# Where an expert's code converts the next expert's weights: six of eight pieces inside the arms of its branch, the third block's place, and two PSUM banks

## The chip, the core and the metric

One core of one Trainium2 chip runs the whole program. The metric is device microseconds of one execution. TensorE (PE) does matrix products into PSUM, VectorE (DVE) and ScalarE (ACT) read PSUM and convert, GpSimd (POOL) gathers and scatters rows by an index list, SyncE (SP) issues the loads of weights.

## What is computed

Chunked attention, a dense layer with `h * sigmoid(1.702 h)`, and a mixture of experts, on 1536 tokens of 512 features. Only the last part matters here:

```python
logits = x @ w_gate                      # 8 experts
expert_idx = np.argmax(logits, axis=1)
gate_w = probs[np.arange(N), expert_idx]
for i in range(N):                       # up to capacity = 384 tokens per expert
    disp[e, counts[e]] = x[i]
h = np.maximum(np.einsum('ecd,edf->ecf', disp, w1), 0.0)   # w1: 8 x 512 x 1024
y = np.einsum('ecf,efd->ecd', h, w2)                       # w2: 8 x 1024 x 512
out[i] = gate_w[i] * y[expert_idx[i], pos[i]]
```

How many tokens an expert has is known only while the program runs.

## The kernel before

**Experts and blocks.** The experts run one after the other, in the order `EORDER`; "expert 0" below is the first to run, "expert 7" the last. An expert's tokens stand in up to three blocks of 128 rows (0, 1 and the "third", number 2). Evaluated with the reference, the counts in running order are 224, 291, 128, 160, 256, 160, 189 and 128.

**Arms.** `others()` emits the code of experts 1 to 7. A branch on the count chooses the arm: *narrow* (`first_of_narrow`, 129 to 192 tokens: experts 3, 5, 6), *wide* (`wide_two`, 193 or more: experts 1 and 4), *lone* (`first_of_one`, up to 128: experts 2 and 7). The wide arm may run a third block (`third`), itself wide or small (up to 64 rows); of experts 1 to 7 only expert 1 has one, a small one with 35 rows. Expert 0 has code of its own (`after_first`). All engines take these branches; an arm's code that is not taken lies between the branch and its target. The arms stand in the order narrow, wide (with the third block's arms inside), lone, and the code that follows them is `next_trans` (PE transposes the next expert's two blocks, L879; ACT and DVE copy them to `xs`, L883 and L884), a second branch that sends block 1's output (`send_second`), `tail(0)` (PE's last 15 products of block 0) and `send(0)`.

**Weights.** A product in float32 is made of three passes over parts `hi` and `lo`, so each expert's w1 and w2, loaded as eight pieces of 512 KB (pieces 0 to 3 are w1, 4 to 7 are w2) into eight buffers `raw`, has to be converted: ACT writes `hi` (L311), DVE writes `lo = raw - hi` (L316) and so frees the buffer, and SP then starts the load of the same piece of the expert after next (L257). While expert e runs, the pieces of e+1 are converted. Six slots `w` hold converted weights, two pieces each: four slots belong to the running expert, so pieces 0 to 3 fit at once, and pieces 4 to 7 only after `w1_done()` has given back the running expert's two w1 slots.

**Where pieces are converted before.** Three of them (`KEEPS[0]`) inside each arm: in the narrow and wide arms behind feature chunks 1, 3 and 5 (`PUMPS`) of the eight chunks of layer 1, in the lone arm through `pump(0..3)`. The other five stand in `steps(1)`, behind `next_trans()` and ahead of the branch with `send_second`.

**Order.** `turned()` and `in_order()` fix the order on PE, ACT and DVE inside one stretch of code, `as_written()` that of the experts' outermost level. Code in one arm that stands in no such stretch, or in two different ones, is free for the scheduler to interleave. Each engine runs its own list in order; layer 1's results pass through four PSUM tiles of kind `h`.

**Narrow arm.** Per chunk: PE makes one PSUM tile (8 products, L1149 and L1151), ACT copies its low half (L1156), DVE adds (L1157), ACT and DVE make `hT` (L1137, L1138), POOL copies block 1's part to `hp` (L1140). Then come 9 products of block 0 (`head`, L1037) and 16 of block 1 that read `hp` (`small2`, L972).

Of the kernel before, what the change touches and what calls it, by code (L numbers as in the profile page):

```python
# [21 lines left out]
P = 128  # L22
# [10 lines left out]
FROM = 150  # L33
EV1 = 2
PUMPS = (1, 3, 5)
RAWS = 4
RT = (4, 7)
LOADS = 1000
# [1 line left out]
EARLY = 12  # L40
KEEP = 4
KEEPS = (3, 8, 8)
HEAD2 = 3
HALF = P // 2
PUMPS1 = (0, 1, 1, 0)
# [46 lines left out]
def kernel(  # L92
# [34 lines left out]
    F2 = F // P  # L127
# [721 lines left out]
    def expert_parts(e, ep, tp, cnt):  # L849
# [79 lines left out]
            flat = t.rearrange("p z c n -> p (z c n)")  # L929
            return flat[:, :flat.shape[1] // 2].rearrange("p (c z n) -> p c z n", z=2, n=HALF)  # L930

        def small_h(b):

            x = narrow(xs_of(b)[0])
            h = narrow(hT_of(b))
            with in_order():
                ps = psum("h", "pst")
                for c in range(KC):
                    nc.tensor.transpose(ps[:, c * HALF:(c + 1) * HALF], xr[b][:HALF, c * P:(c + 1) * P], ident[:HALF, :HALF])
                pv = ps[:, :KC * HALF].rearrange("p (c n) -> p c n", n=HALF)  # L940
                nc.scalar.activation(out=x[:, :, 0], in_=pv, func=AF.Copy)
                nc.vector.tensor_tensor(out=x[:, :, 1], in0=pv, in1=x[:, :, 0].bitcast(F32), op=ALU.subtract)
                hs = []
                for j in range(2):
                    w_tile(("w1", e, j), 0)
                    w = w_tile(("w1", e, j), 1)
                    ps = psum("h", "psh")
                    for wz in range(2):
                        for c in range(KC):
                            nc.tensor.matmul(ps, lhsT=x[:, c].rearrange("p z n -> p (z n)"), rhs=w[:, wz, c, :],  # L950
                                             start=(wz, c) == (0, 0), stop=(wz, c) == (1, KC - 1))
                    hs.append(ep.tile([P, 512], F32, tag="hs", name="hs", bufs=2))
                    nc.scalar.activation(out=hs[j], in_=ps, func=AF.Copy)
                for j in range(2):
                    ps = psum("h", "psu")
                    for c in range(KC):
                        nc.tensor.matmul(ps[:, c * HALF:(c + 1) * HALF], lhsT=hs[j][:, c * P:(c + 1) * P], rhs=pair,
                                         start=True, stop=True)
                    hi, lo = (h[:, 4 * j:4 * j + 4, z] for z in range(2))
                    pv = ps[:, :KC * HALF].rearrange("p (c n) -> p c n", n=HALF)  # L960
                    nc.scalar.activation(out=hi, in_=pv, func=AF.Relu)
                    nc.vector.scalar_tensor_tensor(out=lo, in0=pv, scalar=0.0, in1=hi.bitcast(F32),
                                                   op0=ALU.max, op1=ALU.subtract)
# [62 lines left out]
        def y_of(b):  # L1026
            if b not in ys:
                ys[b] = psum(("y", "yl", "h")[b], "psy")
            return ys[b]
# [49 lines left out]

        begun = []  # L1080

        def begin():

            then = w_apart(e, KEEPS[0])
            if then is not None:
                begun.append(then)

        def end():

            if begun:  # L1090
                begun.pop(0)()

        def head(b):

            layer2_part(b, y_of(b), range(HEAD2))

# [4 lines left out]
        def first_of_one():  # L1101

            def pump(i):
                if i < 2:
                    begin()
                if i > 1:
                    end()

            with in_order():
                turn = block_h(0, pump)  # L1110
                begin()
                layer2_part(0, y_of(0), range(HEAD2 - 1))
                turn()
                end()
                layer2_part(0, y_of(0), range(HEAD2 - 1, HEAD2))

        def first_of_two():

            with turned():
                for fc in range(F2):  # L1120
                    layer1(fc)
                    end()
                    if fc in PUMPS:
                        begin()
                head(0)
                layer2_part(1, y_of(1), range(F2))

        def first_of_narrow():

# [12 lines left out]
            with turned():  # L1142
                for fc in range(F2):
# [14 lines left out]
                    if fc > 0:  # L1158
                        scale(fc - 1)
                    end()  # L1160
                    if fc in PUMPS:
                        begin()
                scale(F2 - 1)
                head(0)
                small2(1)

# [11 lines left out]
        def w1_done():  # L1178
            for j in range(F // 512):
                w_free(("w1", e, j))  # L1180

        def third_first(b, is_wide):

            if is_wide:
                trans(b, "h")
                block_h(b)()
            else:
                small_h(b)

        def third_second(b, is_wide):  # L1190

            gate(b)
            if is_wide:
                layer2_part(b, y_of(b), range(F2))
                send(b)
            else:
                small2(b)
                send_small(b)

        def third(b):  # L1200

            def go(is_wide):
                third_first(b, is_wide)
                ys.pop(b, None)
                third_second(b, is_wide)

            with tc.If(cnt[ex] > b * P):
                both(cnt[ex] > b * P + HALF, lambda: go(True), lambda: go(False))

        def wide_two():  # L1210

            first_of_two()
            third(2)

        def send_second(wide):

# [5 lines left out]
        def after_first():  # L1222

            y_of(0)
            with tc.If(cnt[E] < P) as some:
                load(0)
                trans(0)
                gate(0)
                block(0)
            with some.Else():  # L1230
                skip(0)
            gate(1)
            for b in range(2, NCB):
                load(b)
            first_of(1)
            assert NCB == 3
            y_of(1)
            hT_of(2)
            xs_of(2)
            third(2)  # L1240
            w1_done()
            layer2_part(1, y_of(1), range(F2))
            steps(1)
            send(1)

        def others():

            assert NCB == 3
            for b in range(2):
                y_of(b)  # L1250
                gate(b)
            for b in range(2, NCB):
                load(b)
                hT_of(b)
                xs_of(b)
            both(cnt[ex] > P, lambda: both(cnt[ex] < P + HALF + 1, first_of_narrow, wide_two), first_of_one)
            w1_done()
            next_trans()
            steps(1)
            with tc.If(cnt[ex] > P):  # L1260
                both(cnt[ex] > P + HALF, lambda: send_second(True), lambda: send_second(False))
            tail(0)
            send(0)

# [196 lines left out]
    with ExitStack() as st:  # L1461
# [4 lines left out]
        ps3 = st.enter_context(tc.tile_pool(name="ps_y", bufs=1, space=PSUM))  # L1466
        ps_pools["y"] = (ps3, "y", [P, 512])
        ps_pools["yl"] = (ps3, "yl", [P, 512])
        for kind in ("y", "yl"):
            psum(kind, "first")  # L1470
        ps2 = st.enter_context(tc.tile_pool(name="ps_h2", bufs=4, space=PSUM))
        ps_pools["t"] = (pst, "t", [P, 512])
# [104 lines left out]
```

## Time and profile before

| | us |
|---|---|
| median of 3 runs | 536.1 (534.67 to 537.48) |
| the profiled execution | 535.17 |
| its span, first to last instruction | 533.4 |
| PE busy in the span | 503.1 (94%) |
| DVE, ACT, POOL busy | 315.4, 277.3, 124.9 |
| stretch of experts 1 to 7 in the span | 365.5 to the end |

A wait in the profile is idle time of an engine and the event that ended it. "issue" means that the engine waited for nothing that the profile shows. [...]

### The profile page before, as it was taken

How to read it: one execution, taken by the hardware profiler on the slowest of the kernel's cores; microseconds unless marked ns; L12 is line 12 of the kernel's file. 1: busy time of each engine (PE TensorE's matmuls, PEld its weight loads, DVE VectorE, ACT ScalarE, POOL GpSimd, SP SyncE). 2: the span in 40 equal slices, each digit the busy share in tenths (PEclk: the TensorE clock that was granted, in tenths of full speed). 3: DMA queues.
4: the chain of work that ended last, by engine and by line, in shares of the span. 5: the costliest groups of instructions: out<-in, count | busy, mean ns of one | idle time of the engine just before them, and what ended most of it. 6: DMA issues, size and time to landing. Idle time of an engine off the chain costs nothing. (4 is left out here: it accounts for less than half of the span.)

```text
span 533.4 us, 10652 instructions
## 1 busy us (share of the span) xinstructions
PE 503.1 (94%) x4085; PEld 432.2 (81%) x4085; DVE 315.4 (59%) x637; ACT 277.3 (52%) x577; POOL 124.9 (23%) x131
## 2 busy tenths in 40 slices
PE   8799999999999999999999999999999979978885
PEld 3589789888998899989988888779887858867763
DVE  3999884588893282322256445538338848475761
ACT  2698886856652352222255334448328745465551
POOL 3245442332410031000000000153012822241402
PEclk9899999999999999999999999999999999999899
DMA  8788655041440004000059301499618958484401
GB/s 317 280 306 293 217 179 180 1 158 58 174 147 20 0 2 159 0 1 1 15 164 292 112 37 40 134 324 340 211 28 278 374 173 276 162 282 144 154 26 49
DMA packets 39155, 81.43 MB, mean 153 GB/s; under 512 B 3945, under 2 KB 10089, under 8 KB 39082
## 3 DMA queue, kind: packets, MB, share of 16 engines
q1 hardware_dynamic: 36010, 70.66, 38.9%
q0 software_dynamic: 3072, 9.80, 5.4%
q8 instruction: 45, 0.74, 0.6%
q14 instruction: 28, 0.23, 0.1%
HBM read 70.96 MB, written 9.75 MB: 151 GB/s over the span
## 5 line engine op out<-in xcount | busy, mean ns | idle before, releaser
L580 PEld LDWEIGHTS psh<-xT,w 128*128 128x128 f32 x1152 | 147.0, 188 | 8.2 <-ACT g L599 0.6
L623 PE MATMUL acc<-w,g 128*128 128x512 f32 x576 | 153.0, 400 | 0.0
L580 PE MATMUL psh<-xT,w 128*128 128x256 f32 x1152 | 151.7, 280 | 0.1
L623 PEld LDWEIGHTS acc<-w,g 128*128 128x128 f32 x576 | 100.6, 188 | 19.5 <-issue 2.1
L595 ACT ACTIVATE sg<-psh 128x256 f32<-128x256 f32 x96 | 36.7, 383 | 126.9 <-PE psh L580 126.4
L603 DVE TENSOR_TENSOR g<-sg,g 128x256 fp32r<-128x256 f32 x78 | 38.1, 490 | 80.3 <-ACT g L599 77.6
L316 DVE TENSOR_TENSOR w<-raw,w 128x1024 fp32r<-128x1024 f32 x64 | 75.8, 1222 | 5.8 <-ACT hs L1001 3.3
L311 ACT ACTIVATE w<-raw 128x1024 fp32r<-128x1024 f32 x64 | 64.5, 1055 | 0.1
L1037 PE MATMUL psy<-w,hT 128*128 128x512 f32 x240 | 59.7, 398 | 0.3
L1037 PEld LDWEIGHTS psy<-w,hT 128*128 128x128 f32 x240 | 43.9, 188 | 10.5 <-issue 0.9
L634 DVE SCALAR_TENSOR_TENSOR x<-acc,x 128x512 f32<-128x512 f32 x36 | 24.1, 685 | 20.8 <-PE acc L623 20.8
L599 ACT ACTIVATE g<-psh 128x256 fp32r<-128x256 f32 x96 | 36.2, 379 | 0.0
L1149 PE MATMUL psh<-xs,w 128*128 128x384 f32 x96 | 30.3, 354 | 3.9 <-DVE low L1157 3.9
L860 POOL DMA_INDIRECT xr<-rows,taker x23 | 28.6, 1245 | 12.6 <-issue 6.1
L758 POOL DMA_INDIRECT y<-rows,taker x1 | 1.2, 1219 | 123.8 <-DVE cnt_i L765 123.8
L884 DVE TENSOR_TENSOR xs<-pst,xs 128x512 fp32r<-128x512 f32 x14 | 9.0, 685 | 34.6 <-ACT xs L883 34.6
L883 ACT ACTIVATE xs<-pst 128x512 fp32r<-128x512 f32 x14 | 7.6, 596 | 38.8 <-PE pst L879 38.8
L1151 PE MATMUL psh<-xs,w 128*128 128x256 f32 x96 | 27.8, 289 | 0.0
L316 POOL TENSOR_TENSOR w<-w,w 128x512 fp32r<-128x512 f32 x12 | 16.6, 1387 | 44.0 <-ACT w L311 44.0
L1043 POOL DMA_INDIRECT out_dram<-y,taker x10 | 14.2, 1422 | 52.7 <-ACT y L1042 22.9
L281 ACT ACTIVATE w<-raw 128x512 f32<-128x512 f32 x32 | 21.3, 675 | 9.7 <-DMA raw<-in_w_out_dram 7.5
L306 POOL TENSOR_TENSOR w<-w,rest 128x512 int32<-128x512 int32 x13 | 17.4, 1338 | 36.3 <-DVE w L292 30.1
(163 smaller groups left out, 695.2 us busy)
## 6 DMA issues: line engine op xcount, KB each, us to landing
raw<-in_w_dram SPq DMA_DIRECT2D x64, 512.0 KB, 6.8
raw<-in_w_out_dram SPq DMA_DIRECT2D x16, 512.0 KB, 4.7
raw<-in_w_in_dram SPq DMA_DIRECT2D x16, 512.0 KB, 4.6
vt<-in_v_dram SPq DMA_DIRECT2D x12, 512.0 KB, 5.9
kt<-in_k_dram SPq DMA_DIRECT2D x12, 368.0 KB, 7.2
qt<-in_q_dram SPq DMA_DIRECT2D x12, 256.0 KB
out_dram<-blank SPq DMA_DIRECT2D x12, 256.0 KB, 2.7
rows<-x SPq DMA_DIRECT2D x5, 520.0 KB, 4.7
```

What stands on the lines that cost most here:

```text
L311: nc.scalar.activation(out=w_dst(self.name, self.i, 0), in_=w, func=AF.Copy)
L316: eng.tensor_tensor(out=lo, in0=w, in1=hi.bitcast(F32), op=ALU.subtract)
L580: nc.tensor.matmul(ps, lhsT=w[:, wz, c, i * P:(i + 1) * P], rhs=xT[tb][:, xz, c, :], start=n == 0, stop=n == 3 * KC - 1)
L595: nc.scalar.activation(out=sg_t[u], in_=h_t[u], func=AF.Silu, scale=1.702)
L599: g_last[:1] = [nc.scalar.activation(out=g[:, 0], in_=h_t.pop(u), func=AF.Silu, scale=1.702).ins]
L603: lo = eng.tensor_tensor(out=g[:, 1], in0=sg_t.pop(u), in1=g[:, 0].bitcast(F32), op=ALU.subtract)
L623: nc.tensor.matmul(acc_t[tb][s], lhsT=g[:, gz, s * P:(s + 1) * P], rhs=w[:, wz, wi, :], start=i == 0 and n == 0, stop=u == last_of(k, tb) ...
L634: nc.vector.scalar_tensor_tensor(out=dst, in0=acc_t[tb][s], scalar=1 / 1.702, in1=dst, op0=ALU.mult, op1=ALU.add)
L860: return nc.gpsimd.indirect_dma_start(out=t, out_offset=None, in_=rows[:, :], in_offset=bass.IndirectOffsetOnAxis(ap=taker[:, b, ex:ex + 1 ...
L1037: nc.tensor.matmul(ps, lhsT=h[:, hz, fc, o:o + P], rhs=w[:, wz, fc % 4, :], start=fc == 0 and n == 0, stop=fc == F2 - 1 and n == 2)
L1149: nc.tensor.matmul(ps[:, :2 * n].rearrange("p (z n) -> p z n", z=2), lhsT=w[:, 0, c, f0:f0 + P], rhs=t[:, :, c, :n], start=c == 0, stop=False)
L1151: nc.tensor.matmul(ps[:, :2 * P], lhsT=w[:, 1, c, f0:f0 + P], rhs=t[:, 0, c, :], start=False, stop=c == KC - 1)
```

## The change

- `PUMPS_N`: in the narrow arm only chunks 3 and 5 start a piece; behind the last chunk `w1_done()` and `more(IN_TWO)` convert pieces 2 to 5, ahead of `head(0)` in the text. Six pieces stand in that arm.
- The wide arm keeps its three pieces in layer 1 and has `more(IN_TWO)` at its end, pieces 3 to 5, in the same `turned()` as the last 15 products of block 1.
- The lone arm has four pieces (`IN_ONE`); two more stand in the new Else of the branch around `send_second`, which a lone expert takes.
- `steps(1)` (now two pieces) moves behind that branch.
- `third` gets an Else: the first 9 products of block 1 (`between`) run in whichever of its three arms is taken; in the wide and small ones behind the block's transposes.
- The PSUM banks of `y` and `yl` are swapped, by the order in which they are first taken.

```diff
+PUMPS_N = (3, 5)
+IN_TWO = 6
+IN_ONE = 4
...
-        def small_h(b):
+        def small_h(b, between):
...
                 nc.vector.tensor_tensor(out=x[:, :, 1], in0=pv, in1=x[:, :, 0].bitcast(F32), op=ALU.subtract)
+                between()
...
-        def begin():
-            then = w_apart(e, KEEPS[0])
+        def begin(keep=IN_TWO):
+            then = w_apart(e, keep)
             if then is not None:
                 begun.append(then)
+            return then
...
+        def more(keep):
+            while begin(keep):
+                if len(begun) > 1:
+                    end()
+            while begun:
+                end()
...
         def first_of_one():
             def pump(i):
-                if i < 2:
-                    begin()
-                if i > 1:
+                if i in (1, 2, 3):
                     end()
+                if i in (0, 1, 2):
+                    begin(IN_ONE)
             with in_order():
                 turn = block_h(0, pump)
-                begin()
+                begin(IN_ONE)
...
                 layer2_part(0, y_of(0), range(HEAD2 - 1, HEAD2))
+            w1_done()
...
                     if fc in PUMPS:
                         begin()
+                end()
                 head(0)
-                layer2_part(1, y_of(1), range(F2))
...
-                    if fc in PUMPS:
+                    if fc in PUMPS_N:
                         begin()
                 scale(F2 - 1)
+                w1_done()
+                more(IN_TWO)
                 head(0)
                 small2(1)
...
+        def third(b, between):
             def go(is_wide):
+                if is_wide:
+                    trans(b, "h")
+                    between()
+                    block_h(b)()
+                    gate(b)
+                    layer2_part(b, y_of(b), range(F2))
+                    send(b)
+                else:
+                    small_h(b, between)
+                    gate(b)
+                    small2(b)
+                    send_small(b)
+                ys.pop(b)
-            with tc.If(cnt[ex] > b * P):
-                both(cnt[ex] > b * P + HALF, lambda: go(True), lambda: go(False))
+            both(cnt[ex] > b * P, lambda: both(cnt[ex] > b * P + HALF, lambda: go(True), lambda: go(False)), between)
         def wide_two():
             first_of_two()
-            third(2)
+            third(2, lambda: layer2_part(1, y_of(1), range(HEAD2)))
+            w1_done()
+            with turned():
+                more(IN_TWO)
+                layer2_part(1, y_of(1), range(HEAD2, F2))
...
-            third(2)
+            third(2, lambda: layer2_part(1, y_of(1), range(HEAD2)))
             w1_done()
-            layer2_part(1, y_of(1), range(F2))
+            layer2_part(1, y_of(1), range(HEAD2, F2))
...
-            both(cnt[ex] > P, lambda: both(cnt[ex] < P + HALF + 1, first_of_narrow, wide_two), first_of_one)
-            w1_done()
+            before = w_state()
+            with tc.If(cnt[ex] > P) as some:
+                both(cnt[ex] < P + HALF + 1, first_of_narrow, wide_two)
+            two = w_state()
+            w_back(before)
+            with some.Else():
+                first_of_one()
+            one = w_state()
             next_trans()
-            steps(1)
-            with tc.If(cnt[ex] > P):
-                both(cnt[ex] > P + HALF, lambda: send_second(True), lambda: send_second(False))
+            w_back(two)
+            with tc.If(cnt[ex] > P) as some:
+                both(cnt[ex] > P + HALF, lambda: send_second(True), lambda: send_second(False))
+            two = w_state()
+            w_back(one)
+            with some.Else():
+                more(IN_TWO)
+            assert w_state() == two
+            steps(1)
             tail(0)
             send(0)
...
-        for kind in ("y", "yl"):
+        for kind in ("yl", "y"):
             psum(kind, "first")
```

What this does to the engines' lists is shown at three places.

**DVE, from the copies of `next_trans` on, expert 3.** `xs` are the next expert's transposed rows, `w` with `raw` is a piece's `lo`, `y` the output of block 1 of a narrow expert. Before:

```order
L884 TENSOR_TENSOR xs_6198<-pst_6758,xs_6198 128x4x128
L884 TENSOR_TENSOR xs_6198<-pst_6765,xs_6198 128x4x128
L316 TENSOR_TENSOR w5_4521<-raw1_3_3365,w5_4521 128x1024
L316 TENSOR_TENSOR w3_97<-raw2_0_4525,w3_97 128x1024
L316 TENSOR_TENSOR w3_97<-raw2_1_4526,w3_97 128x1024
L316 TENSOR_TENSOR w2_96<-raw2_2_4527,w2_96 128x1024
L316 TENSOR_TENSOR w2_96<-raw2_3_4528,w2_96 128x1024
L1260 COMPARE_AND_BRANCH
L1170 COMPARE_AND_BRANCH
L1170 UNCONDITIONAL_BRANCH
L978 TENSOR_SCALAR y_6794<-psy_6208,gt_6212 64x512
L979 SCALAR_TENSOR_TENSOR y_6794<-psy_6208,gt_6212,y_6794 64x512
```

After, from the second copy on:

```order
L887 TENSOR_TENSOR xs_6288<-pst_6894,xs_6288 128x4x128
L1277 COMPARE_AND_BRANCH
L1186 COMPARE_AND_BRANCH
L1186 UNCONDITIONAL_BRANCH
L982 TENSOR_SCALAR y_6908<-psy_6298,gt_6302 64x512
L983 SCALAR_TENSOR_TENSOR y_6908<-psy_6298,gt_6302,y_6908 64x512
L1186 UNCONDITIONAL_BRANCH
L319 TENSOR_TENSOR w3_97<-raw2_0_4525,w3_97 128x1024
L319 TENSOR_TENSOR w3_97<-raw2_1_4526,w3_97 128x1024
L1277 UNCONDITIONAL_BRANCH
L319 TENSOR_TENSOR w2_96<-raw2_2_4527,w2_96 128x1024
L319 TENSOR_TENSOR w2_96<-raw2_3_4528,w2_96 128x1024
```

Five pieces stood between the copies and the output `y`; now `y` follows the copies, a lone expert's two pieces stand in the other arm, and two pieces follow the branch.

**ACT, the beginning of the wide arm, expert 3's code (each expert has the same).** `w` with `raw1_3` is `hi` of piece 3, `raw1_0` and `raw1_1` those of pieces 0 and 1. Before:

```order
L1170 UNCONDITIONAL_BRANCH
L915 ACTIVATE hT_6199<-psh_6373 128x256
L915 ACTIVATE hT_6199<-psh_6388 128x256
L311 ACTIVATE w0_94<-raw1_0_3362 128x1024
L915 ACTIVATE hT_6199<-psh_6404 128x256
L915 ACTIVATE hT_6199<-psh_6421 128x256
L311 ACTIVATE w0_94<-raw1_1_3363 128x1024
```

After:

```order
L1186 UNCONDITIONAL_BRANCH
L314 ACTIVATE w5_4521<-raw1_3_3365 128x1024
L918 ACTIVATE hT_6289<-psh_6472 128x256
L918 ACTIVATE hT_6289<-psh_6487 128x256
L314 ACTIVATE w0_94<-raw1_0_3362 128x1024
L918 ACTIVATE hT_6289<-psh_6503 128x256
L918 ACTIVATE hT_6289<-psh_6520 128x256
```

Piece 3, in the text at the arm's end, has moved to the arm's first place, on ACT and likewise on DVE and in SP's list of loads. Pieces 4 and 5, which need the slots of `w1_done()`, stand behind the third block.

**PE, the small arm of the third block, expert 1.** `pst` are the transposes, `psy_4966` is block 1's output, `psh` layer 1 of the third block. Before:

```order
L1170 UNCONDITIONAL_BRANCH
L939 MATMUL pst_5364<-ident_64,xr_4955 128x64 x4
L950 MATMUL psh_5371<-w0_94,xs_4960 128x512 x8
L950 MATMUL psh_5382<-w5_4521,xs_4960 128x512 x8
L957 MATMUL psu_5393<-pair_88,hs_5380 128x64 x4
```

After:

```order
L1186 UNCONDITIONAL_BRANCH
L942 MATMUL pst_5376<-ident_64,xr_4973 128x64 x4
L1041 MATMUL psy_4966<-w3_97,hT_4957 128x512 x9
L954 MATMUL psh_5392<-w0_94,xs_4978 128x512 x8
L954 MATMUL psh_5403<-w5_4521,xs_4978 128x512 x8
L961 MATMUL psu_5414<-pair_88,hs_5401 128x64 x4
```

Nine products of block 1 now stand between the transposes and the layer 1 that waits for their copies.

## Rows read from the trace of the kernel before

**Rows 1.** Page: span, then two groups of section 5 (busy us, mean ns).

```profile
span 533.4 us, 10652 instructions
...
L316 DVE TENSOR_TENSOR w<-raw,w 128x1024 fp32r<-128x1024 f32 x64 | 75.8, 1222 | 5.8 <-ACT hs L1001 3.3
L311 ACT ACTIVATE w<-raw 128x1024 fp32r<-128x1024 f32 x64 | 64.5, 1055 | 0.1
```

**Rows 2.** Stretches of experts 1 to 6: length, busy by engine, PEclk, DMA share, GB/s.

```profile
365.50:400.10 34.60, 33.67 (x206) 29.48 (x205) 15.99 (x29) 13.91 (x29) 5.18 (x5) 1.00 0.50 169
400.10:413.98 13.88, 13.10 (x65) 10.52 (x64) 11.91 (x17) 12.34 (x21) 4.20 (x3) 1.00 0.89 280
413.98:438.75 24.77, 20.22 (x114) 17.71 (x112) 16.66 (x31) 14.34 (x32) 13.73 (x15) 1.00 0.78 283
438.75:463.82 25.07, 23.99 (x153) 21.27 (x152) 15.23 (x25) 12.36 (x24) 5.91 (x5) 1.00 0.65 215
463.82:489.35 25.53, 20.42 (x113) 17.62 (x112) 15.83 (x31) 14.62 (x33) 7.18 (x12) 1.00 0.65 207
489.35:514.62 25.27, 21.70 (x113) 19.01 (x112) 17.72 (x33) 14.65 (x33) 7.34 (x11) 0.93 0.38 131
```

**Rows 3.** Waits of PE, 340 to 533: total us, times, longest.

```profile
PE pst L879 <- issue: 7.3, 3, 3.6
PE psh L1149 <- DVE low L1157: 3.9, 3, 1.8
PE psy L972 <- POOL hp L1140: 1.8, 1, 1.8
PE psh L912 <- DVE hT L916: 0.9, 1, 0.9
PE psh L950 <- DVE xs L942: 0.9, 1, 0.9
PE psy L1049 <- ACT y L839: 0.8, 1, 0.8
PE psu L1006 <- ACT hs L1001: 0.8, 1, 0.8
```

**Rows 4.** Timeline of DVE, beginning of expert 3: start, us, instruction.

```profile
412.71 5.76 DVE L316 TENSOR_TENSOR w<-raw,w 128x1024 fp32r<-128x1024 f32 x5
...
419.32 0.62 DVE L1157 TENSOR_TENSOR low<-psh,low 128x192 f32<-128x192 f32 x2
```

**Rows 5.** Timeline, end of expert 3's arm: idle before in brackets.

```profile
429.19 0.29 POOL L1140 CAST hp<-hT 128x128 fp32r<-128x128 f32 x1 [0.27 <-DVE hT L1138]
...
434.28 1.06 PE L879 MATMUL pst<-ident,xr 128*128 128x128 f32 x8 [3.58 <-issue]
```

**Rows 6.** DMA queues within 430.5 to 434.5: packets, MB, share.

```profile
q8 instruction: 1, 0.02, 1.8%
```

**Rows 7.** Timeline of POOL, expert 4's sends and expert 5's copies.

```profile
466.78 2.05 POOL L1043 DMA_INDIRECT out_dram<-y,taker  x1 [9.82 <-ACT y L1042]
475.94 1.00 POOL L1043 DMA_INDIRECT out_dram<-y,taker  x1 [7.11 <-ACT hT L1137]
...
478.39 1.95 POOL L1140 CAST hp<-hT 128x128 fp32r<-128x128 f32 x8
```

**Rows 8.** Timeline of PE: expert 4's third-block branch; end of expert 5's arm.

```profile
451.39 1.33 PE L1037 MATMUL psy<-w,hT 128*128 128x512 f32 x5
452.87 6.77 PE L1037 MATMUL psy<-w,hT 128*128 128x512 f32 x28
...
484.94 1.07 PE L879 MATMUL pst<-ident,xr 128*128 128x128 f32 x8 [2.20 <-issue]
```

**Rows 9.** Timeline of PE, layer 1 of expert 1.

```profile
365.49 11.61 PE L912 MATMUL psh<-xs,w 128*128 128x256 f32 x96
```

**Rows 10.** Load issues of SP, 363.1 to 364.3.

```profile
L257 SPq DMA_DIRECT2D raw<-in_w_dram x1: 368/368/368, 364.1 to 364.1; - x1
```

**Rows 11.** DMA queues, 346.5 (first of these loads) to 369.0: packets, MB, share.

```profile
q1 hardware_dynamic: 2431, 4.70, 61.7%
```

More of the change, by code (lines that the diff above doesn't have):

```diff
@@ L1180, in w1_done @@
                 w_free(("w1", e, j))
[L1182 to L1200, printed above, removed]
-            def go(is_wide):
-                third_first(b, is_wide)
-                ys.pop(b, None)
-                third_second(b, is_wide)
-            with tc.If(cnt[ex] > b * P):
-                both(cnt[ex] > b * P + HALF, lambda: go(True), lambda: go(False))
+        def third(b, between):
+            def go(is_wide):
+                if is_wide:
[12 more added lines that the diff above has]
+            both(cnt[ex] > b * P, lambda: both(cnt[ex] > b * P + HALF, lambda: go(True), lambda: go(False)), between)
         def wide_two():
             first_of_two()
-            third(2)
+            third(2, lambda: layer2_part(1, y_of(1), range(HEAD2)))
[3 more added lines that the diff above has]
+                layer2_part(1, y_of(1), range(HEAD2, F2))
         def send_second(wide):
```

## The prediction

> **What bounds the kernel now.** I read the page first: a span of 533.4 us [rows 1], with PE busy for 94% of it by the table above. So only time in which PE idles can go, and the change touches experts 0 to 7 alone. The stretches by expert [rows 2] show where PE idles: subtracting its busy time from the length gives 0.9 us in expert 1, 1.1 in expert 4, 0.8 in expert 2, but 4.6, 5.1 and 3.6 in experts 3, 5 and 6, the three with a narrow arm; in expert 6 the granted clock is 0.93 besides. PE's waits [rows 3] give the causes, 16.4 us in all:
>
> - 3.9 us in three waits for DVE's first sums, at the start of experts 3, 5 and 6, the longest 1.8 (expert 6). DVE works through five pieces (5.76 us, so 1.15 each) before it reaches the first L1157 [rows 4], while PE fills the four PSUM tiles and stops. Expert 4 loses 0.9 in the same way (L916), expert 2 loses 0.8 because `hs` on ACT comes late behind five pieces of its own.
> - 1.8 us for POOL's `hp` in expert 5. Expert 4's second output is issued at 466.78 [rows 7], since ACT made its `y` only behind five pieces; the next send follows at 475.94, and the copies that PE wants start at 478.39.
> - 7.3 us "issue" at L879, the transposes behind the narrow arms: 3.58 [rows 5], 2.20 [rows 8], so some 1.5 in expert 6. Within expert 3's gap one 16 KB packet of queue q8, kind "instruction", moves [rows 6] (0.02 MB in the row). The branch out of a narrow arm jumps over the wide and the lone arm: by the listing 274 products of two instructions each, 548. I take the gap for the fetch of code. It begins when PE's sequencer has got past its last wait, POOL's last `hp`: that ends at 429.48 [rows 5] and 480.34 [rows 7], and PE resumes 4.80 and 4.60 us later, at 434.28 and 484.94. Of these PE still covers some with queued products.
> - 0.9 us for the third block's `xs` in expert 1, and 0.8 us in expert 0 for `y` of the block before (L1049), which lies in the bank that its dummy product writes.
>
> **The change part by part.** No product is added or taken away; pieces stay 64. So the sum consists of waits.
>
> *Fewer pieces at an expert's start.* Behind a narrow or wide arm DVE has two pieces instead of five between the copies and the next layer 1: 3 x 1.15 = 3.5 us earlier, more than any of the waits that it ends. Expert 4 gains 0.9, expert 5 1.1, expert 6 1.8. In a wide arm piece 3 comes in front, which leaves a net two pieces less (2.3), still enough for expert 4's 0.9. Behind a lone arm (expert 3) four pieces instead of five remain, 1.15 us against a wait of 0.97 (3.9 - 1.8 - 1.1): I take 0.7, between 0 and 1.0. Expert 2 gains its 0.8: ACT has two pieces (2 x 1.06 [rows 1]) where it had five. Its fourth piece in the arm stands between `turn(0)` and the second `hs`, where PE has six products to cover it.
>
> [...]
>
> *The send in front of the pieces.* `y` of block 1 no longer waits for five pieces, so expert 4's send is issued some 5 us earlier (5 x 1.06), and its successor, the gather and the copies with it. Expert 5 gains its 1.8 whole.
>
> *The narrow arm's end.* One piece less inside the loop and fewer ahead of it let DVE's last `hT`, and so the last `hp`, follow PE's last product of layer 1 more closely. In expert 3 PE ended its arm at 434.28 - 3.58 = 430.70, 1.2 us behind the last `hp`. Two pieces less on DVE are 2.3 us, PE itself comes 0.7 to 1.0 earlier, so the fetch begins some 1.5 us earlier in relation to PE's work: 1.6 gained of 3.58, bounds 0 and 2.2. The same for experts 5 (0.8 of 2.20) and 6 (0.6 of 1.5). The four pieces behind the loop take DVE 4.6 us and ACT 4.2, beside the 25 products of `head` and `small2` (5.8 us at 0.24 each) and the gap that remains: they end about when the transposes do. I cost them at nothing. If the cover is gone (the gap vanishes), the copies of `xs` start up to 1 us late, and `tail(0)`, 15 products or 3.6 us, still lies between them and layer 1.
>
> *The loads.* A piece converted earlier starts its load earlier. Between 400 and 414 DMA is 0.89 busy [rows 2], before that 0.50; so the shift goes into idle time. An expert wants 8 x 0.52 = 4.2 MB, 15 us at 280 GB/s [rows 2], and the six experts there last 24.9 us on average. The one place where this fails is piece 3 in front of expert 1's wide arm. Its buffer's load is issued at 364.1 [rows 10] as the ninth since 346.5; nine pieces are 4.72 MB, and q1 has moved 4.70 MB by 369.0 [rows 11]. With a little for the landing, ACT can convert it at 370.2, and everything on ACT's list waits, the first `hT` too. ACT ends at 371.3, DVE at 372.5, DVE's first `hT` at 372.9. PE has four PSUM tiles at 11.61 / 8 = 1.45 us [rows 9] and stops at 365.49 + 5.80 = 371.3. So **a new wait of 1.6 us**, bounds 0 (had the load been quicker) and 4. In expert 4 that load is some 5 us old by then, and nothing waits.
>
> *Third block.* In expert 1 nine products (2.2 us) now cover the 0.9 us: gained whole.
>
> *Banks.* Expert 0's 0.8 us may go, but expert 1's new wait is set by a transfer in a busy queue and takes back whatever is gained ahead of it. I count 0.
>
> *Lone entry.* The code of a lone arm is fetched under `tail(0)`; with more transfers beside it I take 0.4 as lost, bounds 0 and 0.8.
>
> [...] The branch past the third block (experts 0 and 4) now jumps over 122 products, 244 instructions, where it jumped over 208; 208 cost 452.87 - 452.72 = 0.15 us [rows 8]. [...]
>
> **The sum.** Expert 1: -1.6 + 0.9 = -0.7. Expert 2: +0.8. Expert 3: 0.7 + 1.6 = 2.3. Expert 4: 0.9. Expert 5: 1.1 + 1.8 + 0.8 = 3.7. Expert 6: 1.8 + 1.7 + 0.6 = 4.1. Lone entries: -0.4. Together 10.7 us gained. The profiled execution took 535.17 us, 1.8 more than its span, and would come to 524.5; the median of the three runs is 0.9 above it, so I forecast 536.1 - 10.7 = 525.4 us.
>
> **The rivals.**
>
> - *The waits move to the narrow arm's end.* The four pieces there issue four loads just when code is fetched, and hold ACT and DVE when the transposes come. Then the 7.3 us of "issue" stay (3.0 less gained), and so does the lower clock (1.7): 536.1 - 6.0 = 530.1. For it: expert 3's fetch, beside busy DMA, took 4.8 us. Against it: expert 5's took 4.6 with DMA less busy, so traffic matters little, and DVE's list gets shorter ahead of the last `hT`.
> - *Slower: the longer jump past the third block is out of reach.* Its place is the branch in experts 0 and 4. There PE has at most a few products queued, so each would cost a whole fetch, 4.7 us, and a stall of that size could bring the lower clock with it, 1.7 as in expert 6: 2 x 6.4 = 12.8, 536.1 - 10.7 + 12.8 = 538.2. It decides if the code that PE holds ahead ends between 208 and 244 instructions. For it: somewhere between 208 and 548 the reach ends. Against it: 244 is near the lower end. [...]
> - *It does not do what it says:* the sums at an expert's start wait for something else than the pieces (the second branch's join, say), the starts keep the 4.5 counted above (0.7, 0.9, 1.1, 1.8) and the clock its 1.7, while expert 1's loss remains: 536.1 - 10.7 + 6.2 = 531.6. DVE is busy until just before [rows 4], so I give it little.
> - *Expert 1's new wait brings the lower clock:* 1.7 more, 527.1; within the range.
>
> **How the numbers follow.** The forecast has 0.65 (the lower clock in expert 1 among it), the first rival 0.18, the slower one 0.07, the last but one 0.07; 0.03 for what I do not see. The range reaches down to 521.5 (expert 1 does not wait: 1.6; the gaps shrink by 1.5 to 2 us more, as their bounds allow) and up to 531.5, the first rival with 1.4 for a longer wait in expert 1 or at a lone entry. Half a per cent is 2.7 us, about what a measurement of this kernel can tell from no change. Faster by more than that (below 533.4) 0.86, within it 0.07, slower 0.07.
>
> **What would show it right or wrong.** In the waits of PE after: no L1149 or L916 counterpart at the starts of experts 4, 5, 6, at most 0.4 in expert 3; no `hp` wait; none for `hs` in expert 2; "issue" at the transposes of some 4 us in all instead of 7.3; a new wait of layer 1 in expert 1, of 1 to 3 us, with ACT idle until a `raw` lands; clock 1.00 in expert 6. Stalls right behind expert 0's or 4's third-block branch would show the slower rival, "issue" of 7 us the first one.

## The result and the profile after

The change made the kernel slower by 0.7%: 540.68 us in the median of 18 runs, against 536.16 us of 18 runs of the kernel before, a ratio of 1.0067 with a 95% interval of 1.0042 to 1.0092. The ratios here leave out runs in which the chip was in a slower state (two of these 18), so they differ a little from the quotients of the medians. The forecast was 525.4 us, with a range of 521.5 to 531.5. The profiled execution took 537.89 us, 2.7 more than that of before, where the sum had promised 10.7 less.

The page's first line and its two groups of piece instructions answer [rows 1]; the pieces cost what they did.

```profile
span 536.1 us, 10692 instructions
...
L319 DVE TENSOR_TENSOR w<-raw,w 128x1024 fp32r<-128x1024 f32 x64 | 76.1, 1219 | 19.0 <-ACT w L314 18.8
L314 ACT ACTIVATE w<-raw 128x1024 fp32r<-128x1024 f32 x64 | 65.1, 1052 | 11.6 <-PE psy L1041 4.4
```

The page also has the queue that brings code: 46 transfers with 0.75 MB, so 16 KB each.

```profile
q8 instruction: 46, 0.75, 0.6%
```

The waits of PE from 340 us to the end (total us, times, longest) answer [rows 3].

```profile
PE psy L1041 <- issue: 6.9, 3, 3.6
PE pst L882 <- issue: 3.0, 2, 1.7
PE psh L915 <- DVE hT L919: 2.8, 1, 2.8
PE psh L915 <- ACT ex L892: 1.3, 1, 1.3
PE psh L1001 <- ACT ex L892: 1.3, 1, 1.3
PE pst L882 <- PE psy L976: 0.9, 1, 0.9
PE psy L1053 <- ACT y L842: 0.8, 1, 0.8
PE psh L1001 <- PE psy L1041: 0.8, 1, 0.8
PE psh L1163 <- DVE low L1171: 0.5, 1, 0.5
```

The reader is to see two things. What the change aimed at is gone: the waits for DVE at the starts fell from 4.8 us to the last row's 0.5, those for `hp` (1.8), `hs` (0.8) and the third block's `xs` (0.9) have no row any more, and the transposes behind the narrow arms (L882: 3.0 and 0.9) wait 3.9 instead of 7.3. That is 4.3 + 1.8 + 0.8 + 0.9 + 3.4 = 11.2 us gained. But there are new waits, the largest on top: 6.9 us of "issue" in front of L1041, products of layer 2 whose operands had long been there. Then come 2.8 us in expert 1 (L915) and 3.4 us at the entries of arms (L915 with 1.3, L1001 with 1.3 and 0.8).

The timeline of PE shows where (start, us, instruction, in brackets the idle time before it and what ended it). It has the second half of expert 1's layer 1, the entry of expert 4's wide arm, the products on both sides of expert 4's third-block branch, and the middle of expert 5's last layer, `tail(0)`.

```profile
373.62 7.31 PE L915 MATMUL psh<-xs,w 128*128 128x256 f32 x48 [2.82 <-DVE hT L919]
...
440.56 11.70 PE L915 MATMUL psh<-xs,w 128*128 128x256 f32 x96 [1.33 <-ACT ex L892]
...
452.10 1.33 PE L1041 MATMUL psy<-w,hT 128*128 128x512 f32 x5
456.56 6.75 PE L1041 MATMUL psy<-w,hT 128*128 128x512 f32 x28 [3.13 <-issue]
...
484.39 1.07 PE L882 MATMUL pst<-ident,xr 128*128 128x128 f32 x8 [1.30 <-issue]
485.21 1.63 PE L1041 MATMUL psy<-w,hT 128*128 128x512 f32 x6
490.40 4.21 PE L1041 MATMUL psy<-w,hT 128*128 128x512 f32 x9 [3.56 <-issue]
```

Behind the third-block branch PE now stops for 3.13 us, where it took 0.15 before [rows 8]. At 490.40 it stops for 3.56 us between the sixth and the seventh of fifteen products that follow each other with no branch between them. In both gaps one transfer of the queue "instruction" ends shortly ahead of the resumption (at 455.0 and 489.1, so 1.5 and 1.3 us ahead), as in [rows 6]; this is the one of 486.5 to 490.5:

```profile
q8 instruction: 1, 0.02, 1.5%
```

The stretches of experts 1 to 6 (columns as in [rows 2]) say what the clock did.

```profile
364.94:399.36 34.42, 31.60 (x190) 27.93 (x189) 16.25 (x28) 12.95 (x28) 6.13 (x5) 0.95 0.53 183
399.36:413.31 13.95, 13.15 (x68) 10.55 (x66) 9.03 (x14) 10.70 (x19) 4.48 (x4) 1.00 0.70 220
413.31:439.24 25.93, 23.78 (x130) 20.42 (x127) 22.41 (x39) 18.98 (x37) 13.28 (x16) 1.00 0.90 302
439.24:463.93 24.69, 20.24 (x137) 18.45 (x138) 12.30 (x20) 10.21 (x20) 6.75 (x5) 1.00 0.79 262
463.93:490.40 26.47, 21.61 (x121) 18.91 (x120) 20.57 (x36) 17.81 (x36) 10.74 (x13) 0.98 0.59 191
490.40:517.00 26.60, 24.87 (x121) 21.55 (x121) 16.83 (x33) 15.19 (x34) 9.06 (x12) 0.89 0.24 77
```

The granted clock, a share of full speed, fell in expert 1 (0.95) and on both sides of the border between experts 5 and 6 (0.98, 0.89), each time with one of the new gaps. Two shorter windows show the stretches at the lower level (granted 0.52 and 0.51), 10.2 us in all; the third line is the one such stretch of before, 3.4 us at 0.50. At the lower level a pair of products of a narrow arm's layer 1 (L1163, L1165) starts 0.53 us after the one before it (494.41, 494.94), behind the stretch 0.30 us (496.33, 496.63).

```profile
373.30:376.70 3.40, 3.08 (x14) 3.08 (x15) 2.39 (x5) 1.72 (x5) 0.00 (x0) 0.52 1.03 380
489.40:496.20 6.80, 5.80 (x16) 4.93 (x17) 1.94 (x6) 1.06 (x5) 2.22 (x1) 0.51 0.79 267
...
497.40:500.80 3.40, 3.40 (x15) 3.40 (x14) 3.26 (x8) 3.26 (x10) 0.39 (x1) 0.50 0.24 88
```

### The profile page after: what moved, and what is told of

Same layout as the page of the kernel before. It is cut to its first block, busy times and chain, and to the rows that moved or that the text cites. A ratio compares the mean times of both kernels' runs of the same rounds, so it can differ in the third digit from the quotient of the medians.

```text
span 536.1 us, 10692 instructions
## 1 busy us (share of the span) xinstructions
PE 505.2 (94%) x4085; PEld 434.6 (81%) x4085; DVE 316.3 (59%) x637; ACT 279.0 (52%) x577; POOL 133.2 (25%) x131
## 5 line engine op out<-in xcount | busy, mean ns | idle before, releaser
L1041 PE MATMUL psy<-w,hT 128*128 128x512 f32 x240 | 62.0, 408 | 6.9 <-issue 6.9
L1041 PEld LDWEIGHTS psy<-w,hT 128*128 128x128 f32 x240 | 45.0, 194 | 17.7 <-issue 8.0
L1163 PE MATMUL psh<-xs,w 128*128 128x384 f32 x96 | 29.6, 347 | 0.5 <-DVE low L1171 0.5
L915 PE MATMUL psh<-xs,w 128*128 128x256 f32 x192 | 24.9, 292 | 4.1 <-DVE hT L919 2.8
L915 PEld LDWEIGHTS psh<-xs,w 128*128 128x128 f32 x192 | 24.5, 200 | 4.8 <-DVE hT L919 3.0
L1165 PE MATMUL psh<-xs,w 128*128 128x256 f32 x96 | 27.3, 285 | 0.0
L295 DVE SCALAR_TENSOR_TENSOR w<-raw,w 128x512 int32<-128x512 int32 x32 | 24.8, 783 | 0.3
```

Of the source, the lines that this page charges most:

```text
L915: mm = nc.tensor.matmul(ps, lhsT=w[:, wz, c, f0:f0 + P], rhs=t[:, xz, c, :], start=m == 0, stop=m == 3 * KC - 1)
L1041: nc.tensor.matmul(ps, lhsT=h[:, hz, fc, o:o + P], rhs=w[:, wz, fc % 4, :], start=fc == 0 and n == 0, stop=fc == F2 - 1 and n == 2)
L1163: nc.tensor.matmul(ps[:, :2 * n].rearrange("p (z n) -> p z n", z=2), lhsT=w[:, 0, c, f0:f0 + P], rhs=t[:, :, c, :n], start=c == 0, stop=False)
L1165: nc.tensor.matmul(ps[:, :2 * P], lhsT=w[:, 1, c, f0:f0 + P], rhs=t[:, 0, c, :], start=False, stop=c == KC - 1)
```

## What was tried, and what came out

Three theories stood. **Code:** the new gaps are fetches of code that come late, because every expert's code on PE is 36 instructions longer (the nine products stand in three arms of the third block instead of once), which shifts the code against the pieces of 16 KB in which the queue moves it. **Piece 3:** the loss is expert 1's wait and its clock. **Traffic:** the loads and pieces within the arms get in the way of other transfers.

**Longer code in the kernel before.** In the wide arm of the third block, which no expert enters here:

```diff
+                layer2_part(b, y_of(b), range(6))
                 layer2_part(b, y_of(b), range(F2))
```

> The kernel before, with 18 products more (36 TensorE instructions) in the wide arm of the third block, an arm that no expert of this input enters: nothing more is executed, but every expert's TensorE code is as much longer as in the changed kernel. Code theory (the loss is code fetched late, because the longer code of an expert moves the places where 16 KB of code end): TensorE's stalls for code change their places and sizes, seen as idle time that ends 1 to 1.6 us after a 16 KB transfer of queue q8, and the time moves by 2 us or more, most likely up, to 538 to 543 us. Piece theory (the loss is expert 1's wait for the piece taken ahead of the arm) and traffic theory (loads and pieces inside the arms): 536 us as before, ratio within 0.998 to 1.002.

Measured: 540.22 us, ratio 1.0059 (1.0023 to 1.0096). Nothing more is executed and no piece has moved, and a loss as large as the change's is there. The timeline of PE in this kernel, at the transposes behind the narrow arms of experts 3, 5 and 6 and at expert 4's third-block branch:

```profile
434.01 1.94 PE L879 MATMUL pst<-ident,xr 128*128 128x128 f32 x8 [4.51 <-issue]
...
456.69 8.30 PE L1037 MATMUL psy<-w,hT 128*128 128x512 f32 x28 [2.86 <-PEq L1208]
...
491.28 1.94 PE L879 MATMUL pst<-ident,xr 128*128 128x128 f32 x8 [3.15 <-issue]
...
516.23 1.06 PE L879 MATMUL pst<-ident,xr 128*128 128x128 f32 x8 [2.18 <-issue]
```

The gaps of [rows 5, 8] grew from 3.58, 2.20 and 1.5 to 4.51, 3.15 and 2.18, and the 2.86 at the branch are new. So code that is never run cost time here, some 4 us. Piece 3 and the loads are in this kernel as they were, so they have no part in its loss; what they cost in the changed kernel is left open by this.

**Piece 3 behind the last chunk of layer 1**, which leaves none to be made in front of the wide arm:

```diff
-PUMPS = (1, 3, 5)
+PUMPS = (1, 3, 5, 7)
```

> The changed kernel, but the wide arm's piece 3 is made behind the last chunk of layer 1 instead of ahead of the arm. [...] Traffic theory: no gain, or a start of layer 1 that waits for DVE again, 540 to 542 us.

Measured: 537.0 us, ratio 1.0021 (0.9987 to 1.0055). Expert 1's wait is gone, and 3.7 us with it; the gaps of experts 4 (3.57) and 5 (2.92) stayed. The piece theory had forecast 536 to 537 us and the code theory 536 to 538, so the time alone does not part them; the gaps that stayed are the code theory's.

**The third block's code as before**, all else as changed (not shown: the same edit in `wide_two`, the empty `between` for `small_h`, and the call of `between` taken out of the wide arm):

```diff
-            both(cnt[ex] > b * P, lambda: both(cnt[ex] > b * P + HALF, lambda: go(True), lambda: go(False)), between)
+            with tc.If(cnt[ex] > b * P):
+                both(cnt[ex] > b * P + HALF, lambda: go(True), lambda: go(False))
...
-            third(2, lambda: layer2_part(1, y_of(1), range(HEAD2)))
+            third(2)
             w1_done()
-            layer2_part(1, y_of(1), range(HEAD2, F2))
+            layer2_part(1, y_of(1), range(F2))
```

> The changed kernel with the third block's code as it was before (one branch without an else, all 24 products of the second block's layer 2 together behind it), which takes the 36 instructions out of every expert again. Code theory: the 3.13 us at the jump past the third block in expert 4 and the 3.56 us in the middle of expert 5's arm go with their low clock, the 0.9 us of expert 1's third block come back: 540.7 - 6.7 - 3.4 + 0.9 = 531 to 533 us. Piece theory: 541 to 542 us (0.9 lost, the wait of expert 1 stays). Traffic theory: 540 to 542 us, since the loads and the pieces in the arms are the changed kernel's.

Measured: 529.69 us, ratio 0.9896 (0.9856 to 0.9937). 11 us back for one edit, more than the 8 to 10 expected. PE at expert 4's branch (start, us, instruction):

```profile
451.70 1.33 PE L1041 MATMUL psy<-w,hT 128*128 128x512 f32 x5
453.19 5.12 PE L1041 MATMUL psy<-w,hT 128*128 128x512 f32 x21
```

The five products end at 453.03 and the next starts 0.16 later: no gap, and none in expert 5's `tail(0)` either. In expert 0, though, the same branch, which jumps no further than in the kernel before, is now followed by a gap (1.00 us, and 1.74 with both edits below; before it had none):

```profile
358.59 5.83 PE L1041 MATMUL psy<-w,hT 128*128 128x512 f32 x24 [1.00 <-PEq L1214]
```

**Both edits.**

> The changed kernel with both edits: piece 3 behind the last chunk of layer 1, and the third block's code as before. Code theory: 531 to 533 less the 2.8 us wait and its clock, 527 to 529 us. Piece theory: 537 us. Traffic theory: 540 us or more.

Measured: 528.91 us, ratio 0.9868 (0.9801 to 0.9935). The best median of all, 7 us below the kernel before; piece 3 is worth 0.8 us here, which the intervals do not tell from nothing.

**The third block kept as changed, and the code shortened elsewhere.** This tells the length of the code from the order of the work:

```diff
-                    layer2_part(b, y_of(b), range(F2))
+                    layer2_part(b, y_of(b), (0, F2 - 1))
                     send(b)
```

> The changed kernel with the third block kept as the change has it (second block's nine products inside each of its arms), but 18 products taken out of the wide arm of the third block, which no expert of this input enters (for an expert with more than 320 tokens that arm would be wrong). Nothing less is executed; each expert's code is as long as before again. Code theory: the 3.13 us at the jump in expert 4 and the 3.56 us in the middle of expert 5's arm go with the low clock behind them, as in the kernel with the third block's old code, and the 0.9 us of its cover stays: 528 to 531 us. If the order of the third block's work were the cause, and not the length of the code: 540 to 541 us as the changed kernel.

Measured: 531.01 us, ratio 0.9889 (0.982 to 0.9958). 9.7 us gained by leaving out instructions that nobody runs. The order theory is out.

**The place alone.** 22 of the fillers at the program's start (products of 512 columns whose result nobody reads) are cut into four of 128. That adds 66 products of two instructions each, so all later code lies 132 instructions further on, and no jump and no expert gets longer:

```diff
+                cut = 4 if fills[0] < SPLIT else 1
+                fills[0] += 1
+                for _ in range(cut):
...
+                        mm = fill_one(512 // cut)
```

> The changed kernel, with 22 of the filler matmuls at the program's start cut into four of 128 columns each: the same columns, 132 TensorE instructions more ahead of everything else, so all later code lies 132 instructions further on, and no jump and no expert gets longer. Place theory (what counts is where 16 KB of code end within each expert): the stalls of experts 4 and 5 go or move to other lines, the time changes by 2 us or more, 532 to 545 us. Length theory (244 instructions past the third block are too far, and longer experts need more transfers): the same stalls at the same lines, 540.7 us within 1 us.

Measured: 529.4 us, ratio 0.9893 (0.9835 to 0.9952). The changed kernel, its experts' code no longer and no shorter, is 11 us faster than it was, more than the place theory had allowed (532). Its PE around expert 4's branch, the same 244 instructions long:

```profile
447.76 3.40 PE L916 MATMUL psh<-xs,w 128*128 128x256 f32 x27
451.00 7.83 PE L1042 MATMUL psy<-w,hT 128*128 128x512 f32 x33
```

All 33 products are one unbroken row, across the branch. So the length of the jump decides nothing by itself: 244 instructions cost 3.13 us at one place and nothing at another, and expert 0's branch above shows it from the other side.

The kernel with both edits was shifted too, by 132 and by 66 instructions.

> The kernel with both edits (piece 3 behind the last chunk, third block's code as before), shifted by the same 132 instructions. Place theory: its stalls move, the time changes by 2 us or more, more likely up (528.9 had none over 2 us): 529 to 537 us. Length theory: 528.9 us within 1 us.

> The same with half the shift: 11 fillers cut in four, 66 instructions more ahead of everything else. Place theory: another pattern of stalls again, 526 to 537 us, different from the shift by 132. Length theory: 528.9 us within 1 us.

Measured: 530.25 us (0.9879, 0.9812 to 0.9946) and 534.71 us (0.9992, 0.9955 to 1.003). The first is not to be told from the unshifted one, so for it the place theory's 2 us did not come; the second lost 5.8. It has a gap in the middle of the eight transposes behind expert 3's arm:

```profile
434.38 0.86 PE L883 MATMUL pst<-ident,xr 128*128 128x128 f32 x4 [2.25 <-issue]
441.56 1.09 PE L883 MATMUL pst<-ident,xr 128*128 128x128 f32 x4 [6.32 <-issue]
```

**The kernel before at the same shifts, and the changed one at 66.** Was 536 an average place, and 541 a bad one?

> The kernel before, shifted by 132 instructions (22 fillers at the start cut in four), nothing else. Place theory: the stalls of 3.58, 2.20 and 1.47 us behind the three narrow arms change or others come, time 530 to 541 us, not within 1 us of 536. Rival (only the changed kernel's longer code is sensitive to place): 535.5 us within 1 us.

> The kernel before, shifted by 66 instructions. Place theory: 530 to 541 us, another pattern of stalls than unshifted and than shifted by 132. Rival: 535.5 us within 1 us.

> The changed kernel, shifted by 66 instructions. Place theory: between the two placements known (540.7 unshifted, 529.4 at 132) or near them, 529 to 541 us; the mean of the change's three placements lies 3 to 6 us below the mean of the three of the kernel before, since the waits that the change removes stay removed (about 7.5 us by the trace, less 2.8 and 1.7 in expert 1). Rival (the change itself costs, and 132 was one lucky place): 540 us or more, and no lower mean.

> The changed kernel with piece 3 behind the last chunk of layer 1 (second edit alone), shifted by 132 instructions. Place theory: as the shifted changed kernel, 529.4, less what is left of expert 1's wait there, which a stall ahead of it has covered: 526 to 529 us. Piece theory: 4 us below it, 525 us.

Measured: the kernel before took 537.07 us shifted by 132 (1.0031, 1.0005 to 1.0057) and 542.39 us shifted by 66 (1.0123, 1.0084 to 1.0162); the changed one 532.06 us shifted by 66 (0.9923, 0.989 to 0.9956). With piece 3 behind the last chunk and the shift by 132 it was 529.73 us (0.9871, 0.9829 to 0.9913), the same as without that edit: the shifted kernel has a gap of 1.91 us in expert 0's last layer, in which the load of piece 3 lands unnoticed: no wait in expert 1 follows. Expected were 526 to 529, missed by 0.7. The kernel before left the expected 530 to 541 at one shift and moved by little more than 1 us at the other. At 66 it too has a second gap behind four of expert 3's eight transposes, as the kernel with both edits has at that shift:

```profile
434.31 1.09 PE L880 MATMUL pst<-ident,xr 128*128 128x128 f32 x4 [4.87 <-issue]
437.40 1.09 PE L880 MATMUL pst<-ident,xr 128*128 128x128 f32 x4 [2.00 <-issue]
```

The table sets beside each median the idle time that PE, by my reading, spent on fetches in the one profiled execution. I counted gaps of 0.2 us and more, from 340 us on, that end 0.9 to 1.9 us behind the end of a 16 KB transfer of the queue "instruction" (the four gaps of before: 3.58, 2.20, 1.47 and 0.29) and that have no wait for DVE or POOL as their cause.

| kernel | fetch gaps, us | time, us | ratio to before |
|---|---|---|---|
| before | 7.5 | 536.2 | 1 |
| before, shifted by 132 | 8.5 | 537.1 | 1.0031 |
| before, shifted by 66 | 12.7 | 542.4 | 1.0123 |
| before, 18 dead products more | 14.1 | 540.2 | 1.0059 |
| changed | 14.2 | 540.7 | 1.0067 |
| changed, shifted by 66 | 12.4 | 532.1 | 0.9923 |
| changed, shifted by 132 | 9.5 | 529.4 | 0.9893 |
| changed, 18 dead products less | 9.2 | 531.0 | 0.9889 |
| changed, third block's code as before | 8.4 | 529.7 | 0.9896 |
| changed, piece 3 behind the last chunk | 13.8 | 537.0 | 1.0021 |
| the same, shifted by 132 | 11.9 | 529.7 | 0.9871 |
| both edits | 8.9 | 528.9 | 0.9868 |
| both edits, shifted by 132 | 8.4 | 530.3 | 0.9879 |
| both edits, shifted by 66 | 13.1 | 534.7 | 0.9992 |

The time goes with the gaps, though not exactly (one execution's gaps stand beside a median): below 10 us of gaps the variants of the change take 529 to 531 us, with 13 to 14 us 535 to 541, with two in between (12.4, 11.9) at 532 and 530; the kernel before takes 536 to 537 with 7.5 to 8.5 and 540 to 542 with 12.7 to 14.1. Below 10 us of gaps the change is some 7 us ahead, above that by anything from 0 to 10. The limit of 1.9 us matters a little: gaps of 1.0 to 1.5 us at expert 7's entry that end 1.95 to 2.2 us behind such a transfer are left out, and with them four rows would read 14.0 (before, by 66), 10.8 (18 dead products less), 13.0 (piece 3, by 132, which would go badly with its 529.7 us) and 9.5 (both edits, by 132). Over the three places 0, 66 and 132 the ratios average 1.0051 for the kernel before, 0.9961 for the changed one and 0.9913 for the one with both edits. By these means the change is worth 0.9%, some 4.8 us, as expected (3 to 6); and the place where it happened to be put took 5.7 us away (1.0067 - 0.9961 is 1.06%), while the kernel before lay 0.5% better than its own mean. But one kernel's three places lie 1.2% to 1.7% apart, so three are too few to call the 0.9% shown; the two further places below, close to the first, are bad ones too (1.0102 and 1.0058 in one run each).

**What makes a place dear.** The 3.56 us in straight code were still open. A shift by 6 and by 12 instructions (one and two fillers cut in four) tells a border in the code from a chance delay.

> The changed kernel, shifted by 6 instructions (one filler cut in four). Border theory: the stall in the middle of expert 5's last layer comes 6 instructions earlier in the code, so with a weight load and a matmul to each product after three of tail(0)'s products instead of six, its size 3 to 5 us; the time stays at 538 to 542 us. Chance or traffic theory: after six products as before, or gone.

> The changed kernel, shifted by 12 instructions. Border theory: the stall comes right behind the eight transposes, after none of tail(0)'s products, 3 to 5 us; the time stays at 538 to 542 us. Chance or traffic theory: after six products as before, or gone.

Measured, one execution each: 541.14 and 538.75 us. PE behind expert 5's narrow arm, first shifted by 6:

```profile
488.92 1.06 PE L883 MATMUL pst<-ident,xr 128*128 128x128 f32 x8 [1.28 <-issue]
489.78 0.96 PE L1042 MATMUL psy<-w,hT 128*128 128x512 f32 x3
495.34 4.49 PE L1042 MATMUL psy<-w,hT 128*128 128x512 f32 x12 [4.59 <-issue]
```

Then shifted by 12:

```profile
482.96 1.06 PE L883 MATMUL pst<-ident,xr 128*128 128x128 f32 x8 [1.70 <-issue]
490.52 5.82 PE L1042 MATMUL psy<-w,hT 128*128 128x512 f32 x15 [6.50 <-issue]
```

The gap came after six products, then after three, then after none: two instructions to a product, exactly as far as the code was moved. And it grew as it came nearer to the gap ahead of the transposes (1.30, 1.28, 1.70 us): 3.56, 4.59, 6.50 us (the last above the expected 5). So there is a border in the code, which stays where it is while the code moves over it. In these traces the dear border is one that follows soon behind the target of a jump: by my reading PE pays for the target's fetch (the 1.28 to 1.70 us) and, some products later, for the next one; in the changed kernel unshifted a 16 KB transfer ends 1.7 us ahead of the transposes (482.7) and the next 1.3 us ahead of the seventh product (489.1). In the third trace the gap lies between the transposes and `tail(0)`, where PE has the branches around `send_second`; in the other two its 3.56 and 4.59 us lie inside the row of products, with no branch between them. How far apart two borders lie, no run here shows.

## Why the forecast was wrong

**The gains were right.** Removed waits counted 11.0 us in the sum (starts 4.5, `hp` 1.8, `hs` 0.8, `xs` 0.9, narrow ends 3.0); the trace after shows 11.2. Expert 3's start keeps 0.49 where at most 0.4 was named. The narrow ends' part is no accident of the place: the same waits are 4.5 us (shifted by 132) and 6.1 (by 66), against 7.9 and 12.7 in the kernel before at the same shifts. At expert 4's entry the new gap of 1.33 us could hide a wait for DVE; with both edits that gap is 0.32 and the 0.9 stays away. The banks were counted at nothing for a reason that was not needed: the swap did not touch the wait, L1053 waits the same 0.8 us for `y` as L1049 did [rows 3]. (The lower end of the range, 521.5, is a little below what its named parts give, 521.8.)

**Expert 1's wait was right in kind and too small.** 1.6 us were forecast, 2.82 came. ACT waited for the transfer as described and got piece 3 0.7 us later than the 370.2 that I had worked out from the bytes of [rows 11], while PE began expert 1 0.55 us earlier than before (364.94, not 365.49):

```profile
370.86 1.06 ACT L314 ACTIVATE w<-raw 128x1024 fp32r<-128x1024 f32 x1 [4.20 <-DMA raw<-in_w_dram]
```

The lower clock behind it, named as the last rival, came too: 3.08 us of PE's busy time at a granted 0.52, about half of it lost. With the edit that removes the wait the kernel was 3.7 us faster at one place, and no faster where a fetch gap covered it (shifted by 132).

**The step that failed is the cost of the code.** The sum priced it at one point, 0.4 us for lone entries, and put the longer jump and all code that is only pushed further on at nothing; the gaps that are new or longer in the trace after are 0.23 (expert 0), 0.80 and 1.31 (lone entries), 1.33 (expert 4's entry), 3.13 (its third-block branch) and 3.56 (expert 5's last layer), 10.4 us, less the 0.3 at expert 7's entry before. That is 9.7 us more than the 0.4. The clock turned by 5.1: 1.7 were to be won, and 6.8 us more at the lower level (granted about half) cost 3.4 by my estimate. The 1.7 is the 0.07 that expert 6's clock lacked, over its 25.27 us [rows 2]; that it can be won back no run shows, and in the trace after that expert's clock was 0.89 over 26.60 us. With 1.2 more in expert 1 the three make 16.0 us against a miss of 13.4 in the profiled execution (10.7 promised, 2.7 lost); 0.2 of the difference is the larger gain above, 0.55 is expert 1's earlier start, and the other 1.8 or so I cannot place gap by gap (PE idled for 1.3 of the 10.2 us at the lower clock).

**The slower rival had the symptom and the wrong reason.** It had 0.07, forecast 538.2 us and a stall behind the third-block branch, from the length of the jump. The stall came in expert 4 (3.13 us) and hardly in expert 0 (0.23). But the same jump of 244 instructions costs nothing in the kernel shifted by 132. That 244 costs what 208 did was my estimate: no row of before shows the cost of a jump between 208 and 548. What the shifted runs agree with is that the place of the borders in the code counts, which a distance does not tell. How much code PE holds in front of a branch no run here decides; behind the narrow arms, over 548 and 584 instructions, PE stalled in every kernel here (3.58, 2.20 and 1.47 us before, 1.66, 1.30 and 0.86 after). To ask whether 244 is near 208 or near 548 was the wrong question, and in any case it left out the code that the jump only pushes further on.

**The other rivals.** The waits did not move to the narrow arms' end: that "issue" fell from 7.3 to 3.9, within the forecast's "some 4". The change did what it says.

## What to carry to other kernels

Code that is longer by a few dozen instructions, run or not, shifts all code behind it against the borders, and that moved the time by 2% here: 529 to 541 us for the changed kernel, unaltered but for its place (0 to 132 instructions further on). So before an edit of a few us is judged by one build, time it at several places (a handful of cut fillers at the start does it), compare the means, and pick the best place at the end. Three places, as here, tell little below 1%. Duplicating nine products into three arms covered 0.9 us and put 36 instructions into every expert's code; at its own place that cost 11 us, while at 132 the kernel with the duplicates (529.4) was as fast as the one without them and without the wait of piece 3 (530.25).

## What the chip showed that I had not expected

- Gaps of 3.56, 4.59 and (both edits, shifted by 66) 6.32 us between instructions with no branch between them, on the engine that bounds the kernel, with all operands there as far as the profile shows.
- 36 instructions that never run cost 0.6% (1.0059); cutting fillers at the very start, at equal columns, changed the time by 11 us down (changed kernel, 132), 7 us up (kernel before, 66) and 6 us up (both edits, 66).
- The target's fetch and the next one lie 5.5 us apart in the changed kernel (one transfer ends at 482.7, the next starts at 488.2). Why the second one is asked for so late stays open.
- The entry of expert 4's wide arm waits 0.7 to 3.2 us in most of the changed kernels (0.3 with both edits, none with both at 66), behind a transfer of code (in the changed kernel unshifted one ends at 439.0, and PE resumes at 440.56). The kernel before had no such gap there; a wait for DVE followed instead. Why the gap is new is not shown.
